# Attention gradients for 32 batches on one core: two heads of dV stored as 120 and 8 rows in every second batch, and o for two batches at once as 104 and 24 rows

## The chip, the cores and the metric

The kernel runs on one core of a Trainium2 chip. A core has engines that run side by side, each with its own list of instructions: TensorE (PE, with its weight loads PEld), VectorE (DVE), ScalarE (ACT), GpSimd (POOL) and SyncE (SP). SP and POOL also issue DMA transfers between the large memory (HBM) and the core's own memory (SBUF). Sixteen DMA engines carry the packets of all these transfers. The metric is the device time of one execution in microseconds; lower is better.

## The reference

Inputs are q and grad_out with shape (32, 32, 4, 128) and k and v with shape (32, 4, 2048, 128), all bf16. It is grouped-query softmax attention: eight query heads share one of four key/value heads. The outputs are o and the three gradients.

```python
k = jnp.repeat(k, rep, axis=1)                # rep = 8
v = jnp.repeat(v, rep, axis=1)
scores = jnp.einsum("bhqd,bhkd->bhqk", q, k) * scale
p = softmax(scores, axis=-1)
o = jnp.einsum("bhqk,bhkd->bhqd", p, v)
# returned: o, and the gradients dq, dk, dv of o against grad_out
```

With dO for grad_out and delta the row sums of dO times o: dV is p transposed times dO; dP is dO times V transposed; dS is p times (dP minus delta); dQ is dS times K, and dK is dS transposed times Q, both with the scale.

## The kernel before, in words

The unit of work is a batch. Its 32 query heads with 4 rows each are the 128 rows of one tile; its 2048 keys are 16 chunks for each of 128 rows, so that one SBUF row holds 16 keys of each of the four heads. k, v, dK and dV of one batch are each 128 rows x 4 heads x 16 chunks x 128 values, which is 2 MB, and a row of one head is 4 KB long.

A batch is cut into named pieces: `LK` and `LV` load k and v by SP's queue, one transfer of 512 KB a head. `QDT`, `KT0` to `KT7` and `VT0` to `VT7` transpose through TensorE, and DVE copies the result out of PSUM. `Sa`, `Sb` make the scores and their maxima, `EXa`, `EXb` the exponentials on ACT. `NRM` (line 234) sums them on DVE, takes the reciprocal `rinv`, and has GpSimd write the scaled operands `dop` (grad_out times `rinv`) and `qp` (q times the scale), four instructions each (line 231). `ETa`, `ETb` transpose the exponentials, `O` multiplies them with v, scales the result into `o_sb`, stores it, and forms delta. `dPa`, `dPb` form dS, `dSTa`, `dSTb` transpose it, `dQ` makes and stores dq. `dV0` to `dV7` and `dK0` to `dK7` (function `outer`) multiply, and ACT copies each piece into a tile of the batch; when the eighth piece is in, two transfers by GpSimd's queue store the tile, 1 MB and two heads each (line 326). The last batch is stored by halves of the chunks (line 319).

The order of all pieces is written out by hand: `HEAD` for the first iterations, `STEADY` for one iteration in the middle, `TAIL` for the end. An iteration mixes the pieces of three batches: a `-` behind a name means the batch before, `+` the batch after, `+2` the one after that. In the steady iteration of batch b, the instructions of GpSimd come in this order: dop and qp of b (`NRM`), the store of dq of b-1, two stores of dk of b-1, the store of o of b, in every fourth iteration (b = 1, 5, 9, ..., 25) two loads of q and grad_out for four batches (`GROUP`, line 142, called by `LK`), and two stores of dv of b. Then comes dop of b+1.

The program gives each transfer of GpSimd's queue the next of eight semaphores, in rotation, and the transfer waits until the transfer that had that semaphore before, the eighth one back, has landed. GpSimd waits in order: what stands behind such a wait in its list, dop of the next batch too, waits with it. A transfer's semaphore is raised by one by each of the sixteen DMA engines when its share is done; the trace has the time of each of these sixteen steps.

Tiles come from pools: four buffers for dV and dK together (`out_pool`), three each for `o_sb` and `dq_sb` (`io_pool`).

## Time and profile before

| what | value |
|---|---|
| median of three runs | 701.2 us (699.08, 701.2, 701.52) |
| the profiled execution | 698.71 us |
| its span, from the first instruction to the last | 696.7 us |
| mean granted TensorE clock | 0.98 |
| PE busy, DVE busy, ACT busy | 90%, 84%, 82% of the span |
| POOL busy | 43% of the span |
| moved by DMA | 274.44 MB, mean 394 GB/s |
| POOL's transfers, from issue to landing (median) | dv 23.6 us, dk 22.1 us, o 23.2 us, dq 16.2 us |
| SP's transfers, from issue to landing (median) | k 13.8 us, v 18.6 us |

The profile is a page made from one execution. It has the busy time of each engine, the span in 40 slices with the bytes per second that were moved, the DMA queues, and the chain of work that ended last, followed back from the last instruction. Beside the page, the trace can be asked for the instructions in a window of time, the waits of one engine, and each transfer's issue and landing. In the chain and the timeline the first number is the start in microseconds from the span's start and the second the duration. "q0" are the transfers that GpSimd issued, "q1" those of SP, and "q8" and "q14" fetch the program's own instructions.

### The profile page before, as it was taken

How to read it: one execution, taken by the hardware profiler on the slowest of the kernel's cores; microseconds unless marked ns; L12 is line 12 of the kernel's file. 1: busy time of each engine (PE TensorE's matmuls, PEld its weight loads, DVE VectorE, ACT ScalarE, POOL GpSimd, SP SyncE). 2: the span in 40 equal slices, each digit the busy share in tenths (PEclk: the TensorE clock that was granted, in tenths of full speed). 3: DMA queues.
4: the chain of work that ended last, by engine and by line, in shares of the span. 5: the costliest groups of instructions: out<-in, count | busy, mean ns of one | idle time of the engine just before them, and what ended most of it. 6: DMA issues, size and time to landing. Idle time of an engine off the chain costs nothing.

```text
span 696.7 us, 28064 instructions
## 1 busy us (share of the span) xinstructions
PE 626.0 (90%) x12352; PEld 454.1 (65%) x12352; DVE 584.5 (84%) x992; ACT 569.1 (82%) x673; POOL 302.7 (43%) x506
## 2 busy tenths in 40 slices
PE   5899999999998989979999798998998889998982
PEld 4577776677676656666666676667766677666661
DVE  5999999999997998869988688888988869898960
ACT  0698989899887989869888687887888868888994
POOL 1355443555454435443354424544434543345452
PEclk9999999999999999999999899999999989999997
DMA  9989999999999999999999999999999999999767
GB/s 339 400 317 411 417 415 416 416 413 415 417 415 417 414 417 416 417 409 412 415 415 413 373 397 398 400 410 382 416 416 417 415 340 393 415 414 415 289 257 274
DMA packets 75577, 274.44 MB, mean 394 GB/s; under 512 B 8448, under 2 KB 8448, under 8 KB 75456
## 3 DMA queue, kind: packets, MB, share of 16 engines
q0 software_dynamic: 37536, 138.16, 49.3%
q1 hardware_dynamic: 37920, 134.50, 48.9%
q8 instruction: 96, 1.57, 0.8%
q14 instruction: 25, 0.20, 0.1%
HBM read 136.31 MB, written 136.31 MB: 391 GB/s over the span
## 4 chain that ended last, share of the span: by engine, by line
PE 43%; DMA 33%; ACT 6%; DVE 5%; POOL 5%; issue 5%; SPq 0%; POOLq 0%; DVEq 0%; ACTq 0%
PE banks L181 18%; DMA k_sb<-in_k_dram 15%; DMA out_dram<-dk 12%; PE banks L303 10%; PE banks L264 7%; ACT dv L307 5%; PE banks L248 5%; DMA out_dram<-dv 4%; PE banks L198 3%; POOL dop L231 2%; DMA v_sb<-in_v_dram 2%; DVE kt L183 2%; DVE ds L338 1%; ACT dk L307 1%; POOL qp L231 1%
## 5 line engine op out<-in xcount | busy, mean ns | idle before, releaser
L307 ACT CAST dv<-banks 128x1024 bf16<-128x1024 f32 x256 | 245.5, 1028 | 56.9 <-PE banks L303 56.3
L307 ACT CAST dk<-banks 128x1024 bf16<-128x1024 f32 x256 | 250.7, 1025 | 34.5 <-PE banks L303 23.6
L183 DVE COPY kt<-banks 128x1024 bf16<-128x1024 bf16 x256 | 164.3, 680 | 8.3 <-PE banks L181 8.3
L183 DVE COPY vt<-banks 128x1024 bf16<-128x1024 bf16 x256 | 166.2, 680 | 1.3 <-PE banks L181 0.9
L181 PE MATMUL banks<-ident,k_sb 128*128 128x128 bf16 x2048 | 145.8, 221 | 13.1 <-DMA k_sb<-in_k_dram 8.6
L181 PE MATMUL banks<-ident,v_sb 128*128 128x128 bf16 x2048 | 143.5, 220 | 14.3 <-ACT dv L307 9.7
L231 POOL TENSOR_SCALAR dop<-do_sb,rinv 32x128 bf16<-32x128 bf16 x128 | 76.7, 599 | 181.3 <-PE banks L303 118.9
L181 PEld LDWEIGHTS <-k_sb 128*128 128x128 bf16 x2048 | 120.8, 99 | 41.9 <-issue 31.7
L181 PEld LDWEIGHTS <-v_sb 128*128 128x128 bf16 x2048 | 122.2, 98 | 28.7 <-issue 23.3
L303 PE MATMUL banks<-dop,e 64*128 64x256 bf16 x1024 | 99.3, 276 | 15.1 <-POOL dop L231 11.3
L326 POOL DMA_DIRECT2D out_dram<-dv x62 | 43.7, 709 | 138.0 <-ACT dv L307 67.6
L338 DVE SCALAR_TENSOR_TENSOR ds<-banks,delta,e 128x1024 bf16<-128x1024 f32 x64 | 82.2, 1284 | 17.3 <-PE banks L198 14.3
L303 PE MATMUL banks<-qp,ds 64*128 64x256 bf16 x1024 | 86.4, 272 | 2.1 <-ACT dk L307 1.4
L231 POOL TENSOR_SCALAR qp<-q_sb,srinv 32x128 bf16<-32x128 bf16 x128 | 78.1, 610 | 10.7
L222 ACT ACTIVATE e<-banks,negb 128x1024 bf16<-128x1024 f32 x64 | 70.7, 1111 | 8.6 <-DVE negb L214 8.5
L211 DVE TENSOR_REDUCE m<-banks 128x1 f32<-128x1024 f32 x64 | 75.1, 1215 | 0.9 <-PE banks L198 0.9
L303 PEld LDWEIGHTS <-e 64*128 64x128 bf16 x1024 | 34.0, 94 | 63.1 <-issue 46.7
L250 DVE COPY et<-banks 128x1024 bf16<-128x1024 bf16 x64 | 41.3, 686 | 29.6 <-PE banks L248 29.6
L303 PEld LDWEIGHTS <-ds 64*128 64x128 bf16 x1024 | 42.2, 94 | 28.8 <-ACT dv L307 13.1
L326 POOL DMA_DIRECT2D out_dram<-dk x62 | 44.0, 713 | 13.6 <-DMA out_dram<-dk 13.0
L250 DVE COPY dst<-banks 128x1024 bf16<-128x1024 bf16 x64 | 43.5, 681 | 5.5 <-PE banks L248 3.6
L248 PE MATMUL banks<-ident,ds 128*128 128x128 bf16 x512 | 39.4, 221 | 7.1 <-ACT dk L307 6.8
(39 smaller groups left out, 484.1 us busy)
## 6 DMA issues: line engine op xcount, KB each, us to landing
k_sb<-in_k_dram SPq DMA_DIRECT2D x128, 512.0 KB, 13.8
v_sb<-in_v_dram SPq DMA_DIRECT2D x128, 512.0 KB, 18.6
out_dram<-dv POOLq DMA_DIRECT2D x64, 1024.0 KB, 23.6
out_dram<-dk POOLq DMA_DIRECT2D x64, 1024.0 KB, 22.1
out_dram<-o_sb POOLq DMA_DIRECT2D x32, 32.0 KB, 23.2
out_dram<-dq_sb POOLq DMA_DIRECT2D x32, 32.0 KB, 16.2
q_sb<-in_q_dram POOLq DMA_DIRECT2D x7, 128.0 KB, 21.9
do_sb<-in_grad_out_dram POOLq DMA_DIRECT2D x7, 128.0 KB, 22.0
```

Of the source, the lines that this page charges most:

```text
L181: nc.tensor.transpose(out=ps[:, 4 * hh + j, :], in_=S[which][:, 2 * (i % 2) + hh, 4 * (i // 2) + j, :], identity=ident[:])
L183: nc.vector.tensor_copy(out=S[f"{which}t{i}"][:], in_=ps)
L211: nc.vector.reduce_max(out=S["m"][:, i:i + 1], in_=S[f"s{i}"][1], axis=AX.X)
L222: nc.scalar.activation(out=S[f"e{i}"][:], in_=ps, func=ACT.Exp, bias=S["negb"][:], scale=scale, accum_out=S["l"][:, i:i + 1],)
L231: nc.gpsimd.tensor_scalar(out=t[r, h % 2, :], in0=src[r, :], scalar1=by[r, :], scalar2=None, op0=ALU.mult)
L248: nc.tensor.transpose(out=ps[:, u, :], in_=S[f"{src}{i}"][:, P * u:P * u + P], identity=ident[:])
L250: nc.vector.tensor_copy(out=S[f"{name}{i}"][:], in_=ps)
L264: nc.tensor.matmul(ps[G * h:G * h + G, :], lhsT=S[f"{xt}{c // 8}"][:, c % 8, G * h:G * h + G], rhs=S[kv][:, h, c, :], start=(c == 0), stop ...
L303: nc.tensor.matmul(ps[:, a, :, c, :], lhsT=S[f"{x}{i // 4}"][r, u:u + P], rhs=S[y][r, :, :], start=True, stop=True, tile_position=(2 * G * ...
L307: copy(out=S[name][:, :, 2 * i:2 * i + 2, :].rearrange("p h c d -> p h (c d)"), in_=banks.ap(t).rearrange("p a (j w) -> p (a j) w", j=2),)
L326: store.dma_start(out=dst[b][:, 2 * a:2 * a + 2, :], in_=o[:, 2 * a:2 * a + 2].rearrange("p h c d -> p h (c d)"))
L338: nc.vector.scalar_tensor_tensor(out=S[f"ds{i}"][:], in0=ps, scalar=S["delta"][:], in1=S[f"e{i}"][:], op0=ALU.subtract, op1=ALU.mult,)
```

## The change

Three things change, all in what GpSimd's queue is given.

- dV: in every odd batch (the last one excepted) the second transfer, heads 2 and 3, is cut into one of rows 0 to 119 and one of rows 120 to 127. In batch 0 heads 2 and 3 are stored as two transfers of 120 rows, one a head, and one of 8 rows for both.
- o: from batch 2 on, o of an even batch stays in SBUF, and with the odd batch behind it two transfers store both batches: rows 0 to 103 and rows 104 to 127. Batches 0 and 1 are stored singly as before.
- `io_pool` has two buffers instead of three; the one for o now holds two batches.

Over two steady iterations GpSimd's queue issues 5 transfers in the even one (dq, dk, dk, dv, dv) and 8 in the odd one (dq, dk, dk, o of 104 rows, o of 24 rows, dv, dv of 120 rows, dv of 8 rows), where it issued 6 and 6. The two loads of `GROUP` fall into odd iterations, between o and dv, before and after. In all GpSimd issues 222 transfers instead of 206. The order of the instructions on every engine is otherwise the same, SP's list included, and so are the bytes.

```diff
--- before.py
+++ after.py
@@ -102,7 +102,7 @@
     ds_pool = ctx.enter_context(tc.tile_pool(name="dsp", bufs=2))
     dst_pool = ctx.enter_context(tc.tile_pool(name="dstp", bufs=2))
     out_pool = ctx.enter_context(tc.tile_pool(name="outp", bufs=4))
-    io_pool = ctx.enter_context(tc.tile_pool(name="iop", bufs=3))
+    io_pool = ctx.enter_context(tc.tile_pool(name="iop", bufs=2))
     qd_pool = ctx.enter_context(tc.tile_pool(name="qdp", bufs=2))
     sm_pool = ctx.enter_context(tc.tile_pool(name="smp", bufs=3))
     ps_pool = ctx.enter_context(tc.tile_pool(name="ps", bufs=1, space=bass.MemoryType.PSUM))
@@ -270,14 +270,20 @@
     def O(b):
         S = st[b]
         t, ps = gathered(S, "et", "v")
-        o_sb = io_pool.tile([P, D], BF16, name="o_sb")
-        nc.vector.tensor_scalar(out=o_sb[:], in0=ps, scalar1=S["rinv"][:], scalar2=None, op0=ALU.mult)
-        banks.give(t)
-        store.dma_start(out=o_f[b], in_=o_sb[:])
+        if b % 2 == 0:
+            st["o"] = io_pool.tile([P, 2, D], BF16, name="o_sb")
+        o_sb = st["o"][:, b % 2, :]
+        nc.vector.tensor_scalar(out=o_sb, in0=ps, scalar1=S["rinv"][:], scalar2=None, op0=ALU.mult)
+        banks.give(t)
+        if b < 2:
+            store.dma_start(out=o_f[b], in_=o_sb)
+        elif b % 2:
+            for r in (slice(0, 104), slice(104, P)):
+                store.dma_start(out=o_f[b - 1:b + 1, r].rearrange("w p d -> p w d"), in_=st["o"][r])
         junk = sm_pool.tile([P, D], BF16, name="junk")
         S["delta"] = sm_pool.tile([P, 1], FP32, name="delta")
         nc.vector.tensor_tensor_reduce(
-            out=junk[:], in0=o_sb[:], in1=S["do"], scale=1.0, scalar=0.0,
+            out=junk[:], in0=o_sb, in1=S["do"], scale=1.0, scalar=0.0,
             op0=ALU.mult, op1=ALU.add, accum_out=S["delta"][:],
         )
 
@@ -322,8 +328,16 @@
                 )
         elif S[name + "left"] == 0:
             o = S.pop(name)
+
+
             for a in range(2):
-                store.dma_start(out=dst[b][:, 2 * a:2 * a + 2, :], in_=o[:, 2 * a:2 * a + 2].rearrange("p h c d -> p h (c d)"))
+                parts = [(slice(0, P), slice(2 * a, 2 * a + 2))]
+                if name == "dv" and a and b == 0:
+                    parts = [(slice(0, 120), slice(2, 3)), (slice(0, 120), slice(3, 4)), (slice(120, P), slice(2, 4))]
+                elif name == "dv" and a and b % 2:
+                    parts = [(slice(0, 120), slice(2, 4)), (slice(120, P), slice(2, 4))]
+                for r, h in parts:
+                    store.dma_start(out=dst[b][r, h, :], in_=o[r, h].rearrange("p h c d -> p h (c d)"))
 
     def dV(b, i, copy=nc.scalar.copy):
         outer(st[b], "e", "dop", dv_v, "dv", i, b, copy)
```

## The prediction

> **What bounds the kernel now.** I read the page first, then the busy time by stage, then the chain of waits, GpSimd's timeline, and last the sixteen semaphore steps of each transfer in the trace.
>
> ```profile
> span 696.7 us, 28064 instructions
> ...
> GB/s 339 400 317 411 417 415 416 416 413 415 417 415 417 414 417 416 417 409 412 415 415 413 373 397 398 400 410 382 416 416 417 415 340 393 415 414 415 289 257 274
> ...
> q0 software_dynamic: 37536, 138.16, 49.3%
> q1 hardware_dynamic: 37920, 134.50, 48.9%
> ```
>
> The moved bytes stand on a plateau of 415 GB/s, with dips (373, 340) and a tail. A 4 KB packet takes 159 ns in the trace; sixteen engines of that pace move 412 GB/s, so on the plateau all sixteen work. By stage:
>
> ```profile
> core 0: us, PE busy (x) PEld busy (x) DVE busy (x) ACT busy (x) POOL busy (x), PEclk, DMA share, GB/s
> ...
> 200.00:300.00 100.00, 90.71 (x1807) 65.00 (x1803) 88.33 (x149) 84.61 (x101) 46.00 (x76) 1.00 1.03 415
> ...
> 384.00:408.00 24.00, 20.44 (x366) 14.12 (x363) 15.99 (x28) 15.96 (x20) 9.27 (x16) 0.86 0.98 371
> 557.00:579.00 22.00, 20.16 (x362) 14.94 (x363) 15.09 (x27) 15.45 (x19) 9.40 (x16) 0.85 0.93 339
> ```
>
> In the dips PE, DMA and the granted clock (0.85) fall together. The chain of waits says what happens there:
>
> ```profile
> 534.93 25.95 DMA out_dram<-dv
> ...
> 561.45 0.71 POOL out_dram L326
> 562.16 4.10 issue
> ...
> 566.28 0.72 POOL out_dram L326
> 567.00 0.09 issue
> 567.09 0.60 POOL dop L231
> ```
>
> GpSimd waits for the landing of a store issued 26 us earlier, the eighth one back; the second dv store waits 4.1 us more, and dop of the next batch stands behind it. GpSimd's timeline and PE's show the same at 388 us, in the next iteration with the two q and grad_out loads:
>
> ```profile
> 382.73 0.76 POOL L142 DMA_DIRECT2D q_sb<-in_q_dram  x1 [4.08 <-DMA out_dram<-dk]
> ...
> 388.60 0.71 POOL L326 DMA_DIRECT2D out_dram<-dv  x1 [4.37 <-ACT dk L307]
> 393.42 0.72 POOL L326 DMA_DIRECT2D out_dram<-dv  x1 [4.11 <-DVE kt L183]
> 394.23 2.63 POOL L231 TENSOR_SCALAR dop<-do_sb,rinv 32x128 bf16<-32x128 bf16 x4
> ```
>
> ```profile
> 391.92 1.20 PE L181 MATMUL banks<-ident,v_sb 128*128 128x128 bf16 x16
> 395.55 0.27 PE L303 MATMUL banks<-dop,e 64*128 64x256 bf16 x1 [2.43 <-POOL dop L231]
> 396.91 0.58 PE L303 MATMUL banks<-dop,e 64*128 64x256 bf16 x3 [1.10 <-POOL dop L231]
> ```
>
> The names DVE and ACT in the brackets were long done; dv of 361.71 and 362.40 landed at 388.02 and 393.13.
>
> Why do stores take 26 us? The sixteen steps of one dv store, from its issue to the first, eighth, fifteenth and sixteenth engine: issued at 92.67, 10.3, 12.7, 14.6, 14.7 us; at 254.34, 11.0, 19.0, 21.1, 26.0; at 410.87, 7.2, 8.3, 10.6, 26.5; at 600.73, 7.6, 8.4, 9.9, 26.2. So late in the run one engine of sixteen is some 16 us behind all others. In the stage with loads alone (issues at 8.67 to 17.60 us) the gap between the last two steps stays at 0.80 to 0.81 us; it grows only once stores run.
>
> **The change part by part.** The sum is made for the profiled execution, 698.7 us: span 696.7 and 2.0 around it. It lies 0.4% below the median of 701.2.
>
> *120 and 8 rows.* A 128-row transfer gives each engine 8 rows. I take it that 120 rows go to fifteen engines with 8 each, and one engine gets none. That saves it 8 rows x 2 heads = 16 packets of 4 KB; the 8-row transfer may give 2 back to it. At 159 ns that is 2.2 to 2.5 us per two batches, 33 to 38 us over 15 odd batches. The late engine lacks 16 us by 600 us, and the others ran dry for some 10 us more in the dips (the slices 409 to 382 and 340, 393 lack 242 of 416 GB/s, each 17.4 us). So the dose fits what that one engine lacks, 26 us, if it is the one spared. The other fifteen get at most 2 packets, 0.3 us, per two batches.
>
> What it is worth if so: first, the landing is then that of the fifteenth step. dop's lateness behind rinv after the five late iterations with loads was 1.6, 3.3, 4.3, 1.9 and 2.7 us, 13.7 in sum. Timing the new list by the fifteenth steps of before, I get 3.1, 3.2, 0.8, 0 and 0: 7.2. Second, the pace. dop starts at 199.13 in batch 9 and at 628.85 in batch 29: 429.7 us, 21.5 an iteration. An iteration moves 8.52 MB (four times 2.1 MB and the small ones), at 415 GB/s 20.5 us. Twenty of these and 7.2 us make 417.2, so 12.5 us less. Bounds: 0 (all of it hidden) to 21.5 (20.4 at 418, no stall).
>
> *The row's cost in a 15-way transfer* is not in this trace. A gain is excluded, as no row shows 4 KB in fewer than 159 ns. From above, slowed 4 KB packets at 200 us take 182 to 196 ns: 16 an engine x 28 ns x 15 = 7 us. I take 0, as 95% of the packets keep 159 ns, and keep 7 for the range.
>
> *One more issue.* 0.71 us in odd batches (line 326), one after dv's second store. The time from there to dop is free where nothing waits: the second dv store of batch 15 ends at 342.41, rinv of the next batch is there at 348.4, so 6 us cover 0.71. Without that cover each 0.71 us would reach PE, since dop ends 0.03 to 0.7 us ahead of its first matmul: 15 x 0.71 = 11 us.
>
> *The eight semaphores.* This is the part that speaks against the change. With 5 and 8 transfers (10 with loads) eight back is another transfer. In plain odd batches the 8-row store waits for the second dv store of the batch before; with loads, for the first dk store of its own iteration. In batch 15 that store landed at 350.56 (fifteenth step 341.90), while dop started at 348.60: 3.0 us late with the lag, in time without. In batch 17 dk of 375.62 landed at 398.48 (fifteenth 388.70), with dop due at 389.95: 9.6 us late with the lag, against 4.3 now, and 0.8 without. This is in the 7.2 above. Other waits (SP's list, PE) gain none.
>
> *o for two batches, and two buffers.* Two stores of o become two of other shapes, with the same 256-byte rows. An o buffer is written again three batches after its store, 60 us, a dq buffer after two, 42 us; o lands after 25.8 us and dq after 17.9 at that stage. No cost; the cover goes if a landing exceeds 42 us.
>
> Sum: 698.7 - 12.5 = 686.2; with half the distance to the median, 687 us.
>
> [...]
>
> **The rivals.** *The spared engine is not the late one.* No row names an engine, so nothing proves which share is left out. Then every landing stays at the sixteenth step and the new semaphore waits bite. By before's landings dop is late in batches 9, 13, 17, 21 and 25 by 7.0, 8.6, 9.6, 7.4 and 8.1 us, 40.7 against 13.7: 27 us more, 726 us. Plain odd batches add up to 4.2 each: in all 64.6 against 13.7, 750 us. I take 726, since stalls shorten the queue (22.0 us instead of 26.3 after the stall at 388). It decides once a dv store takes over 27 us, as from 250 us on.
>
> *The lag is cured and nothing is gained.* PE and ACT are 90% and 82% busy, and up to 180 us an iteration took 19.5 us at the same 415 GB/s. If the others' queues merely fill, 15 x 0.71 us of issues and the 7 us eat the 12.5: 698 to 702 us.
>
> *15-way transfers are so slow* that the spared time comes back in other engines: doubling 240 packets' time costs 16 x 159 ns x 15 = 38 us; a part of it is 705 to 720.
>
> **How the numbers follow.** Forecast 0.53: 678 to 695 us, since the dose fits and a whole share is left out. Wrong engine 0.35; nothing gained 0.06; slow transfers 0.06. A measurement here tells 0.5%, 3.5 us, from no change. Faster 0.53, same 0.06, slower 0.41. The range 678 to 728 holds the forecast's cases but 0.03, the third and fourth, and half of the wrong engine's.
>
> **What would show it.** Right: a dv store's fifteenth and sixteenth steps within some 3 us late in the run, landings near 15 us, no "4.10 issue" in front of dop, a plateau to 640 us. Wrong: the last gap still grows to 10 us or more, the 8-row store is issued after rinv of the next batch, and PE idles for dop in every odd iteration. It would also be wrong if 4 KB packets grew beyond 159 ns.

## The result: slower by 1.1%

The changed kernel takes 708.78 us (median of five runs, 705.23 to 710.9) against 700.34 us for the kernel before (699.08 to 701.52). The ratio is 1.0112, with a 95% interval of 1.007 to 1.0153. The prediction said 687 us and faster; the time lies inside its range, but on the other side of no change. The profiled execution took 708.78 us, 706.9 of them the span. Of all runs below, two executions of the kernel called start 1 were in the chip's slower state and are left out of its median and ratio. (One number of the description above has to be put right: GpSimd issues 223 transfers after the change, not 222.)

First the page of the changed kernel. The lines are the span, the bytes per second in forty slices, the two large queues, the shares of the chain that ended last, the group of dV matmuls that wait for `dop`, and the median landings of loads and stores.

```profile
span 706.9 us, 28119 instructions
...
GB/s 339 389 308 389 411 415 416 415 412 415 414 416 410 384 402 380 412 413 416 416 411 414 373 379 402 384 416 409 412 401 369 415 386 407 408 408 413 262 223 264
...
q0 software_dynamic: 38320, 138.17, 49.1%
q1 hardware_dynamic: 37920, 134.50, 48.5%
...
PE 68%; issue 8%; ACT 8%; DVE 5%; DMA 5%; POOL 4%; SPq 0%; POOLq 0%; ACTq 0%; DVEq 0%
...
L309 PE MATMUL banks<-dop,e 64*128 64x256 bf16 x1024 | 101.2, 278 | 25.4 <-POOL dop L231 20.5
...
k_sb<-in_k_dram SPq DMA_DIRECT2D x128, 512.0 KB, 11.2
v_sb<-in_v_dram SPq DMA_DIRECT2D x128, 512.0 KB, 15.7
...
out_dram<-dv POOLq DMA_DIRECT2D x48, 1024.0 KB, 18.4
out_dram<-dv POOLq DMA_DIRECT2D x15, 960.0 KB, 21.8
out_dram<-dv POOLq DMA_DIRECT2D x16, 64.0 KB, 17.9
```

The large transfers land sooner than before: k after 11.2 us (13.8 before), v after 15.7 (18.6), whole dv stores after 18.4 (23.6). The kernel is slower all the same. The slices say where: the plateau of 415 is still there, but it has more holes (384, 402, 380 from 230 us on, 373 and 379 from 389 us on).

The slices can be turned into time. Each slice lacks (416 - GB/s) / 416 of its length. Before the change the first three slices lack 8.0 us, the 34 in the middle 11.0, the last three 17.9; with 274.44 MB at 416 GB/s, 659.7 us, that makes the span of 696.7. After the change it is 9.0, 17.0 and 21.2. So the middle lost 6.0 us and the end 3.3. It also shows something that should have been seen in advance: 11.0 us was all that the middle had to give, and the forecast counted on 12.5.

The stages, by windows (the columns are the stretch, its length, and the busy time of PE, weight loads, DVE, ACT and POOL, then PE's granted clock, the DMA share and GB/s):

```profile
200.00:300.00 100.00, 89.26 (x1792) 64.39 (x1788) 81.49 (x141) 79.86 (x95) 46.45 (x76) 0.95 1.01 400
208.00:232.00 24.00, 16.52 (x296) 12.24 (x294) 17.03 (x28) 14.98 (x19) 8.54 (x13) 0.92 1.02 409
384.00:408.00 24.00, 18.53 (x349) 13.71 (x350) 15.60 (x27) 14.85 (x19) 9.25 (x16) 0.88 0.98 381
557.00:579.00 22.00, 18.35 (x358) 13.56 (x354) 16.01 (x28) 15.86 (x19) 10.39 (x17) 0.94 1.02 402
```

From 200 to 300 us, where the kernel before had no hole (415 GB/s), there is one now. From 208 to 232 us PE is busy for 16.5 of 24 us while the DMA engines are still full; the hole in the bytes follows after that, when the loads that PE's progress would have released are missing (SP's loads of k wait for PE's matmuls by 337.5 us in sum, up to 13.5 at a time). GpSimd's timeline of that stretch (start, duration, engine, line, operation; in brackets the idle time before it and what ended it):

```profile
207.82 0.62 POOL L296 DMA_DIRECT2D out_dram<-dq_sb  x1
208.44 1.42 POOL L340 DMA_DIRECT2D out_dram<-dk  x2
209.86 1.35 POOL L282 DMA_DIRECT2D out_dram<-o_sb  x2
213.86 0.78 POOL L142 DMA_DIRECT2D q_sb<-in_q_dram  x1 [2.65 <-DMA out_dram<-dk]
218.91 0.77 POOL L142 DMA_DIRECT2D do_sb<-in_grad_out_dram  x1 [4.27 <-DMA out_dram<-dv]
225.92 1.47 POOL L340 DMA_DIRECT2D out_dram<-dv  x2 [6.24 <-issue]
229.44 0.57 POOL L340 DMA_DIRECT2D out_dram<-dv  x1 [2.05 <-DMA out_dram<-dk]
230.09 2.62 POOL L231 TENSOR_SCALAR dop<-do_sb,rinv 32x128 bf16<-32x128 bf16 x4
```

The store at 229.44 is the new one of 8 rows. With ten transfers in an iteration that has the loads, the eighth one back is the first dk store of the same iteration, issued at 208.44 and landed at 229.15. `dop` of batch 10 stands behind it. Its input `rinv` was there at 221.62, so `dop` is 8.3 us late; before the change it was 1.6. PE, in the same stretch:

```profile
223.60 1.05 PE L181 MATMUL banks<-ident,v_sb 128*128 128x128 bf16 x16
231.40 0.37 PE L309 MATMUL banks<-dop,e 64*128 64x256 bf16 x1 [6.75 <-POOL dop L231]
232.76 0.58 PE L309 MATMUL banks<-dop,e 64*128 64x256 bf16 x3 [0.99 <-POOL dop L231]
```

That is a stall of 7.7 us where PE had none of more than 2.43 us in the piece shown of before. Added over all iterations, `dop` is late by 22.7 us (13.7 before): 8.3 us in batch 10, 5.8 in 18, 3.5 in 26, 2.0 in 22, 1.9 in 14, 1.1 in 6.

PE's idle gaps of more than 0.15 us between 22 and 650 us, by what ended them:

| PE waits for | before, us | after, us |
|---|---|---|
| `dop` (GpSimd) | 11.3 | 20.5 |
| nothing that the profile shows | 9.5 | 15.1 |
| ACT's copies of dV | 9.3 | 9.8 |
| ACT's copies of dK (an output buffer) | 6.8 | 0.2 |
| loads of k and v | 7.0 | 0.4 |

So the sooner landings did pay: 6.6 us for buffers and 6.6 us for loads are gone. `dop` took 9.2 us back, and the second row 5.6. In all, the rows of the table grew by 2.1 us only, and the span by 10.2. PE's own busy time grew by 3.6 us (626.0 to 629.6), at a granted clock of 0.975 against 0.980, and the rest lies outside the window. By the starts of `dop`, the loss falls between batches 9 and 13 (90.2 us against 84.2) and between 29 and 31 (42.2 against 38.3); between 13 and 17 and between 25 and 29 the changed kernel is the faster one by 2 to 3 us. The gaps of that row end 1.2 to 1.6 us after a 16 KB packet of the queue q8, which fetches instructions. The end of the kernel has one more of them, in the chain (start, duration, what):

```profile
660.52 0.27 PE banks L181 x3
660.80 3.44 issue
664.24 0.89 PE banks L181 x13
```

It too ends 1.4 us after such a packet, and it is about as long as the 3.3 us that the last slices lost.

### The profile page after: what moved, and what is told of

Read it like the earlier page. It is cut to its first block, busy times and chain, and to the rows that moved or that the text cites. A ratio compares the mean times of both kernels' runs of the same rounds, so it can differ in the third digit from the quotient of the medians.

```text
span 706.9 us, 28119 instructions
## 1 busy us (share of the span) xinstructions
PE 629.6 (89%) x12352; PEld 456.2 (65%) x12352; DVE 584.6 (83%) x992; ACT 569.3 (81%) x673; POOL 317.0 (45%) x523
## 2 busy tenths in 40 slices
DMA packets 76361, 274.44 MB, mean 388 GB/s; under 512 B 9337, under 2 KB 9517, under 8 KB 76240
## 4 chain that ended last, share of the span: by engine, by line
PE 68%; issue 8%; ACT 8%; DVE 5%; DMA 5%; POOL 4%; SPq 0%; POOLq 0%; ACTq 0%; DVEq 0%
PE banks L181 28%; PE banks L309 17%; PE banks L264 8%; PE banks L198 7%; PE banks L248 7%; ACT dv L313 6%; DMA out_dram<-dv 3%; POOL dop L231 2%; POOL out_dram L340 2%; DVE kt L183 2%; DVE ds L352 1%; ACT dk L313 1%; DVE vt L183 1%; DVE m L211 1%; DMA v_sb<-in_v_dram 1%
## 5 line engine op out<-in xcount | busy, mean ns | idle before, releaser
L181 PEld LDWEIGHTS <-k_sb 128*128 128x128 bf16 x2048 | 122.4, 99 | 40.9 <-issue 37.0
L340 POOL DMA_DIRECT2D out_dram<-dv x79 | 53.8, 685 | 177.9 <-ACT dv L313 104.5
L309 PE MATMUL banks<-dop,e 64*128 64x256 bf16 x1024 | 101.2, 278 | 25.4 <-POOL dop L231 20.5
L352 DVE SCALAR_TENSOR_TENSOR ds<-banks,delta,e 128x1024 bf16<-128x1024 f32 x64 | 82.2, 1284 | 19.7 <-PE banks L198 17.1
L309 PE MATMUL banks<-qp,ds 64*128 64x256 bf16 x1024 | 88.3, 273 | 2.3 <-ACT dk L313 1.4
L222 ACT ACTIVATE e<-banks,negb 128x1024 bf16<-128x1024 f32 x64 | 70.7, 1110 | 12.2 <-DVE negb L214 12.2
L309 PEld LDWEIGHTS <-ds 64*128 64x128 bf16 x1024 | 43.8, 94 | 28.6 <-ACT dv L313 12.6
L198 PE MATMUL banks<-vt,qdt 128*32 128x512 bf16 x512 | 42.1, 398 | 1.2 <-issue 1.0
## 6 DMA issues: line engine op xcount, KB each, us to landing
k_sb<-in_k_dram SPq DMA_DIRECT2D x128, 512.0 KB, 11.2
v_sb<-in_v_dram SPq DMA_DIRECT2D x128, 512.0 KB, 15.7
out_dram<-dk POOLq DMA_DIRECT2D x64, 1024.0 KB, 16.5
out_dram<-dv POOLq DMA_DIRECT2D x48, 1024.0 KB, 18.4
out_dram<-dv POOLq DMA_DIRECT2D x16, 64.0 KB, 17.9
```

Source lines behind the costliest of these rows:

```text
L181: nc.tensor.transpose(out=ps[:, 4 * hh + j, :], in_=S[which][:, 2 * (i % 2) + hh, 4 * (i // 2) + j, :], identity=ident[:])
L198: nc.tensor.matmul(ps[G * h:G * h + G, a, :], lhsT=S["qdt"][:, col, G * h:G * h + G], rhs=xt[:, 4 * (h % 2):4 * (h % 2) + 4, :].rearrange( ...
L222: nc.scalar.activation(out=S[f"e{i}"][:], in_=ps, func=ACT.Exp, bias=S["negb"][:], scale=scale, accum_out=S["l"][:, i:i + 1],)
L309: nc.tensor.matmul(ps[:, a, :, c, :], lhsT=S[f"{x}{i // 4}"][r, u:u + P], rhs=S[y][r, :, :], start=True, stop=True, tile_position=(2 * G * ...
L340: store.dma_start(out=dst[b][r, h, :], in_=o[r, h].rearrange("p h c d -> p h (c d)"))
L352: nc.vector.scalar_tensor_tensor(out=S[f"ds{i}"][:], in0=ps, scalar=S["delta"][:], in1=S[f"e{i}"][:], op0=ALU.subtract, op1=ALU.mult,)
```

## The experiments

Theory A is the prediction's: the late DMA engine costs time, and sparing it gives time. Its rivals (B, later W and U) say that the extra transfers and their waits, or the uneven shares, decide. All ratios are to the kernel before on the same chip. Executions of one kernel differ by up to 10 us (start 3: 702.06 to 712.55), so what is read from one trace explains where time goes, and the ratios say how much. The runs of the next part were on one chip; starts 1 to 4 on a second; start 5, its variant and the two other kernels behind it on a third; the first four kernels with a moved store on a fourth, and the last two kernels on a fifth.

### The dealing taken back in steps

First, the two 120-row stores of batch 0 go. By the author's count they shift the dealing of all later shares by six (15, 15 and 8 shares are six more than two rounds of sixteen), so without them another engine should be the spared one. That the shares go round in turn was an assumption here.

```diff
-                if name == "dv" and a and b == 0:
-                    parts = [(slice(0, 120), slice(2, 3)), (slice(0, 120), slice(3, 4)), (slice(120, P), slice(2, 4))]
-                elif name == "dv" and a and b % 2:
+                if name == "dv" and a and b % 2:
```

> The changed kernel with dv of batch 0 stored by two transfers of 128 rows again; the cuts of 120 and 8 and of 104 and 24 rows in later batches stay. In the trace of the changed kernel the late engine carries 16 packets of every 120-row transfer (its step comes 4.9 to 5.3 us after that of the transfer before), so it is not the spared one; a 104-row transfer made 13 packets of 4 KB and a 24-row one 12 packets of 1 KB, so the shares go to 13 and 12 engines, and the sum of 15, 8, 13 and 12 is 48, three full rounds. Without the 15 + 15 + 8 of batch 0 the spared engine should be another one, ten further on in the round. Theory A (the spared engine was the wrong one, and the one spared now is the late one): the gap between the fifteenth and the sixteenth step stays under 4 us to the end, 690 us (684 to 697). Theory B (it is still another one): the gap grows to 6 to 10 us as in the changed kernel, 705 to 711 us. Theory C (the late engine is late because of its backlog alone and sparing does nothing): as B.

Measured: 706.59 us (706.08 to 710.55), ratio 1.0103 (1.0071 to 1.0136). The 16th step of a 120-row store comes 4.4 to 6.6 us after that of the transfer before (2.7 in the last), as for a 128-row store; in the changed kernel it is 5.0 us in each of the three read here (issued at 226.63, 265.12 and 309.45 us: 5.03, 4.98, 4.99), against 4.83 to 5.25 for the whole dk and dv stores issued between 208 and 309 us, one of 2.77 aside. The last engine is therefore not the spared one in either. One thing moved: from batch 7 to 27 the last step of the 8-row store now comes 0.64 to 1.14 us after the one before, mostly 0.8 to 0.9, where the changed kernel has 0.40 to 0.49. By these steps the last engine carries two packets of it here and none there. (In the first batches no single engine is clearly last yet, and the steps are mixed in both.)

Second, the same number of transfers, but in halves, meant to give all sixteen engines the same.

```diff
-            for r in (slice(0, 104), slice(104, P)):
+            for r in (slice(0, 64), slice(64, P)):
...
-                    parts = [(slice(0, 120), slice(2, 4)), (slice(120, P), slice(2, 4))]
+                    parts = [(slice(0, 64), slice(2, 4)), (slice(64, P), slice(2, 4))]
```

> The same number of transfers in the same places as in the changed kernel, but cut as 64 and 64 rows (dv of odd batches, o of two batches), and in batch 0 as 128, 64 and 64 rows, so that each engine gets the same number of rows. Theory A (the loss comes from the eight semaphores, as a transfer more in odd batches makes GpSimd wait for later landings, and sparing a wrong engine does nothing): 705 to 713 us, dop of batches 10, 14, 18, 22 and 26 late by 2 to 9 us as in the changed kernel. Rival (the loss comes from transfers over 15, 13, 12 or 8 engines): 699 to 702 us.

Measured: 704.71 us, ratio 1.0053 (1.0019 to 1.0087). `dop` is late by 22.5 us in sum, 6.4 of them in batch 10. The time lies between the two expectations. About half of the loss comes without the uneven cuts, from the transfers alone; the interval overlaps a little with that of the run before.

Third, the part of the change that saves a transfer: o of two batches in one store of 128 rows, dV as before the change.

```diff
-            for r in (slice(0, 104), slice(104, P)):
+            for r in (slice(0, P),):
```

> The part of the change that only lessens the transfers: o of two batches in one transfer of 128 rows, dv stored as before; 11 transfers in two batches instead of 12. Theory A (the rotation of semaphores sets the stalls): the batches with loads wait for a transfer that was issued earlier, so dop is late by less than the 13.7 us in sum of the kernel before, 692 to 699 us. Rival (the number of transfers does not matter): 699 to 702 us.

Measured: 696.91 us (696.45 to 697.25), ratio 0.9952 (0.9934 to 0.9971). It is faster than both kernels, though one engine is late as before, by up to 17.5 us. `dop` is late by 7.5 us in sum. PE's waits (what waited, for what: us in total, times, the longest) show what is next in line:

```profile
PE banks L181 <- DMA k_sb<-in_k_dram: 21.4, 19, 1.9
PE banks L181 <- ACT dv L313: 10.5, 30, 0.5
PE banks L309 <- POOL dop L231: 5.1, 6, 1.1
```

Fourth, `dop`'s stalls taken away by another road: the kernel before with its loads of q and grad_out on SP's queue, so that GpSimd issues six transfers in every iteration.

```diff
-            GROUP(b // W + 1, nc.gpsimd)
+            GROUP(b // W + 1, nc.sync)
```

> The kernel before with the loads of q and grad_out issued by SP's queue instead of GpSimd's, so that no iteration has eight transfers of GpSimd's. It measures what the stalls in the batches with loads cost. Theory A: dop is no longer late in batches 10, 14, 18, 22 and 26 (13.7 us in sum before), 687 to 695 us, and the gap of the last engine still grows past 10 us. Rival (DMA alone is the bound, the stalls only move time): 698 to 702 us.

Measured: 713.57 us (710.41 to 716.37), ratio 1.0195 (1.015 to 1.024). `dop` is late by 0.4 us in the whole run and the gap between the last two engines is at most 5.9 us. Neither expectation held. Both things that the prediction wanted to cure are cured, and the kernel is slower than any other here. PE's waits, and the longest in its timeline:

```profile
PE banks L181 <- DMA k_sb<-in_k_dram: 32.8, 12, 9.1
```

```profile
230.51 0.61 PE L181 MATMUL banks<-ident,k_sb 128*128 128x128 bf16 x4 [9.09 <-DMA k_sb<-in_k_dram]
```

The loads now stand in front of k in SP's list, and PE waits for k instead. So this run does not say what the cures would be worth without that wait.

### Does any start spare the late engine, and does it pay?

If the dealing goes round in turn, each transfer starting at the engine behind the last one's (the cursor), the place of the spared engine can be moved. Four kernels cut o of batch 0 so that, by the author's count, the start should move by one to four from that of the first experiment. That count was an assumption, and the packets of batch 0, below, do not bear it out.

```diff
-            store.dma_start(out=o_f[b], in_=o_sb)
+            for r in (slice(0, 90), slice(90, P)) if b == 0 else (slice(0, P),):
+                store.dma_start(out=o_f[b, r], in_=o_sb[r])
```

The other cuts are 121 and 7, 102 and 26, 114 and 14 rows.

> [...] Theory A (a late engine that is fixed): in exactly one of the four the late engine's step of a 120-row transfer comes within 1 us of the step before it, and its gap stays under 4 us; this one takes 688 to 699 us, the other three 704 to 712. Theory B (the start is not the same in every execution, or another engine becomes late once this one is spared): none of the four is under 702 us.

> [...] Theory A: one of the four has a gap under 4 us and 688 to 699 us. Theory B: all 702 to 712 us.

> [...] Theory A: one of the four has a gap under 4 us and 688 to 699 us. Theory B: all 702 to 712 us.

> [...] Theory A: one of the four has a gap under 4 us and 688 to 699 us. Theory B: all 702 to 712 us.

Measured: 705.7 us (ratio 1.0043 to 1.0143), 707.65 (1.0085 to 1.0134), 709.36 (1.0104 to 1.0156) and 708.35 (1.0064 to 1.0188). In all four the 16th engine carries the 120-row store (4.3 to 6.6 us up to batch 27) and, from batch 7 on, two packets of the 8-row one (0.6 to 0.9 us, mostly 0.8). `dop` of batch 10 is late by 7.6 to 8.6 us in each. In the second the gap between the last two engines is at most 3.4 us after 480 us, and it gains nothing by it.

The fifth start was chosen from these steps: if each cut moves the start as counted, only one place of the late engine fits the 8-row steps of all these kernels, and this start should spare it. It cuts o of batch 0 into 40 and 88 rows. Four kernels ran with it, two of them in the next part.

> The sixth start. In the starts 0, 1, 2, 3 and 4 the late engine carries the 8-row transfer (its last step comes 0.8 us after that of the transfer before), in the changed kernel (start 6) it does not (0.4 us). If the shares are dealt in turn, the 8-row transfer goes to the eight engines from the spared one on; only one engine fits all six traces, and it is the one that start 5 spares. So in this kernel the last step of a 120-row transfer should come less than 1.5 us after the one before, and the 8-row step 0.8 us or more. Theory A (the prediction's: a spared late engine pays for the extra transfers): gap between the 15th and 16th step at most 3 us, dv landing in 15 to 18 us, 687 to 697 us. Theory B (the rotation of eight semaphores and the extra transfers set the loss, and the lag is not what sets the time): the dose fits and the gap shrinks, but dop of batch 10 is still 6 to 9 us late and the time is 703 to 710 us.

Measured: 710.98 us (705.75 to 712.16), ratio 1.0166 (1.0141 to 1.0191). No gain, and the expected step did not come: the 16th engine still carries the 120-row store (4.7 to 5.9 us after the one before, up to batch 27), and 0.6 to 0.8 us for the 8-row one. The gap between the last two is 6.9 us at most. The time is a microsecond above theory B's range.

The packets of batch 0 say why: the start did not move. The 38 rows of start 1 had been counted as two shares. In its trace they are twelve packets of 768 bytes (three rows of 256), one of 516 (two rows and 4 bytes) and three of 12 bytes. That fits the rows divided by 16 and rounded up for each engine, until no rows are left. The cuts of the other starts fit this too: the 40 rows of start 5 are 13 packets of three rows and one with a single row. So these plain stores were shared out otherwise than the strided stores of 120, 104 and 24 rows, and, by the steps that follow, did not move the start.

The later steps agree. In the first experiment and in all five starts the last engine carries the 120-row and the 8-row store, and its step in the 104-row store is mostly 0.35 to 0.38 us, too short for that store's 4 KB share (0.47 to 0.50 us for most o stores of the kernel with dV cut alone, below, where each engine gets 4 KB). By the count of shares, only three engines are in the 8-row store and out of the 104-row one; had the start moved by one to four, these would be three other engines in start 4 than in start 1, which ran on the same chip.

So none of the five starts spared the late engine, and whether sparing it pays was not tested. They are the first experiment over again with one more store in batch 0. These six kernels, on three chips, have ratios of 1.0093 to 1.0166, so differences below 0.7 points between kernels on different chips have to be read with care.

> Start 5 with dq of two batches in one transfer, so that two iterations have 12 transfers again, as before the change (5 and 7 instead of 6 and 6; with loads 9). In iterations with loads the 8-row store still waits for the first dk store of its own iteration. Theory A: the spared engine now costs nothing extra: 684 to 694 us. Theory B: dop of batch 10 still 6 us late or more, 696 to 705 us: some 5 us less than start 5, because four iterations with loads and all plain ones wait for older transfers.

```diff
-        dq_sb = io_pool.tile([P, D], BF16, name="dq_sb")
-        nc.scalar.activation(out=dq_sb[:], in_=ps, func=ACT.Copy, scale=S["srinv"][:])
+        if b % 2 == 0:
+            st["dq"] = io_pool.tile([P, 2, D], BF16, name="dq_sb")
+        nc.scalar.activation(out=st["dq"][:, b % 2, :], in_=ps, func=ACT.Copy, scale=S["srinv"][:])
...
-        store.dma_start(out=dq_f[b], in_=dq_sb[:])
+        if b % 2:
+            store.dma_start(out=dq_f[b - 1:b + 1].rearrange("w p d -> p w d"), in_=st["dq"][:])
```

(A scratch tile, `junk`, gets one buffer instead of three to make room.) Measured: 708.34 us, ratio 1.012 (1.0083 to 1.0158). `dop` of batch 10 is late by 7.2 us, 26.3 in sum. With the transfer count of before the loss is still there, so the count alone is not the cause. (The start did not move in this kernel either.) Both theories expected a lower time.

> o and dq each for two batches in one whole transfer, dV as before the change: 10 transfers in two iterations where there were 12. No engine is spared. Theory B: fewer transfers move the eight-back wait to older ones, dop is late by under 5 us in sum, and the time is 690 to 696 us, at or below that of o pairs alone (696.9). Theory A: the lag still reaches 15 us and more and every landing with it, so no better than o pairs alone: 696 to 702 us.

Measured: 699.95 us, ratio 0.9997 (0.9986 to 1.0009). `dop` is late by 0.4 us in the whole run, as theory B said, yet the kernel is slower than with o in pairs alone. PE's waits for k grow (page, the k transposes: 33.3 us idle, 24.8 with o in pairs alone). The time is in theory A's range, with a lag of 12.2 us at most. Fewer transfers do not go on paying; why k comes later with dq in pairs was not settled.

> dV cut into 120 and 8 rows, with o of two batches in one whole transfer, 12 transfers in two iterations as before the change. The shares of two iterations now add up to 7 more than a whole turn, so the spared engine changes each time, and the late one is spared once or twice in 15 at most. In iterations with loads the 8-row store waits for dq, not dk, of its own iteration, which lands about 5 us earlier. Theory A: no engine is relieved, nothing is gained: 699 to 704 us, with gaps of 8 us or more. Theory B: against o pairs alone (696.9) one more transfer in odd iterations and a wait for dq: 698 to 703 us, dop of batch 10 late by 2 to 5 us. The two agree on the time; apart from theory A, a time at 704.7 us or above would say that uneven dealing as such costs, whatever the rotation.

```diff
                 parts = [(slice(0, P), slice(2 * a, 2 * a + 2))]
+                if name == "dv" and a and b % 2:
+                    parts = [(slice(0, 120), slice(2, 4)), (slice(120, P), slice(2, 4))]
```

Measured: 700.26 us, ratio 1.0004 (0.9988 to 1.002), in the range that both theories gave. Against o in pairs alone, the cut of dV costs 0.5 points. `dop` of batch 10 is late by 1.8 us: here the 8-row store waits for dq of its own iteration, which lands earlier than dk.

The steps of this kernel also bear on how shares are dealt. By the count, two iterations deal seven shares more than whole turns, so the window of eight engines that get the 8-row store should move by seven each time. The last engine's step in the 8-row stores of batches 1, 3, ... 27 comes after the one before by 0.82, 0.40, 0.81, 0.87, 0.48, 0.81, 0.49, 0.84, 0.47, 0.79, 0.49, 0.40, 0.87, 0.47 us. An engine that stands at place 5 of the window in batch 1, then at 14, 7, 0, 9, 2, 11, 4, 13, 6, 15, 8, 1, 10 of sixteen, is inside the window (0 to 7) in just those of the fourteen cases where the step is about 0.8, and outside where it is 0.4 to 0.5. Place 0 is the engine that the 120-row store spares, and in that batch, 7, its step in the 120-row store comes after 2.41 us instead of some 5. So the fourteen steps fit shares of 16, 15 and 8 that are dealt on from where the last ones ended. The place 5 was chosen to fit; no other of the sixteen fits more than twelve. The fifteenth step, of batch 29, is 0.36 us where the count would give 0.8; the queues run empty there (the last three slices of the changed kernel move 223 to 264 GB/s), and in every kernel that step is 0.2 to 0.5. So one engine is last through this run, and it was spared once. That is read from the pattern: the trace names no engine.

### The wait in front of `dop`

The last dv store of an odd batch is now issued behind `dop` and `qp` of the next batch, in four kernels: start 5, the changed kernel, start 5 with dq in pairs, and the even one with halves.

```diff
+    held = []
...
         paired(S, "qp", S["q"], S["srinv"], b)
+        while held:
+            store.dma_start(**held.pop())
...
-                for r, h in parts:
-                    store.dma_start(out=dst[b][r, h, :], in_=o[r, h].rearrange("p h c d -> p h (c d)"))
+                for n, (r, h) in enumerate(parts):
+                    args = dict(out=dst[b][r, h, :], in_=o[r, h].rearrange("p h c d -> p h (c d)"))
+                    if b and n:
+                        held.append(args)
+                    else:
+                        store.dma_start(**args)
```

> Start 5, with the 8-row store issued behind dop and qp of the next batch. Theory A (a spared late engine pays, the wait hid it): dop of batch 10 under 3 us late, 687 to 695 us, clearly below the even kernel of this call. Theory W (the wait in front of dop was the loss, the lag is worth nothing): dop in time likewise, 697 to 702 us, the same as the even kernel. Theory U (uneven shares cost by themselves: seven engines carry 18 packets where 16 is even, 0.32 us in each pair of batches, 4.8 us over 15 pairs): 3 to 5 us above the even kernel.

> The changed kernel with the same move: its spared engine is not the one that is late before the change. Theory A: no relief, 699 to 704 us, above start 5 by 8 us or more. Theory W: 697 to 702 us, the same as start 5 and the even kernel. Theory U: 3 to 5 us above the even kernel, as start 5.

> As start 5 deferred, with dq of two batches in one transfer: 12 transfers in two iterations, as before the change, and the 120-row store waits for one of the iteration before it in iterations with loads, no longer for dq of its own. Theory A: 685 to 692 us. Theory W: 695 to 700 us, near o and dq pairs alone (699.9). Theory U: 700 to 705 us.

> The even kernel (64 and 64 rows, no engine spared, the same transfers) with its last dv store issued behind dop and qp of the next batch. All theories: dop of batch 10 under 3 us late. Theory W: the loss of 3.7 us is gone, 697 to 702 us. If it stays at 703 us or above, the wait in front of dop is not what costs, and the count of transfers is left.

The even kernel first. GpSimd's timeline without the move:

```profile
224.01 1.31 POOL L340 DMA_DIRECT2D out_dram<-dv  x2 [4.68 <-ACT dq_sb L294]
229.12 0.62 POOL L340 DMA_DIRECT2D out_dram<-dv  x1 [3.80 <-DMA out_dram<-dk]
229.82 2.62 POOL L231 TENSOR_SCALAR dop<-do_sb,rinv 32x128 bf16<-32x128 bf16 x4
```

and with it:

```profile
223.86 1.31 POOL L348 DMA_DIRECT2D out_dram<-dv  x2 [4.74 <-ACT dk L317]
225.25 2.62 POOL L233 TENSOR_SCALAR dop<-do_sb,rinv 32x128 bf16<-32x128 bf16 x4
227.96 0.21 POOL L244 TENSOR_SCALAR srinv<-rinv 128x1 f32<-128x1 f32 x1
228.27 2.65 POOL L233 TENSOR_SCALAR qp<-q_sb,srinv 32x128 bf16<-32x128 bf16 x4
230.97 0.67 POOL L247 DMA_DIRECT2D out_dram<-dv  x1
```

`dop` starts at 225.25 instead of 229.82, still 3.7 us late where under 3 was expected. In the changed kernel it is 5.3 us late, in start 5 6.3, in start 5 with dq in pairs 3.5: where o is two stores and dq one a batch, the store of dv in front of `dop` is now the ninth and waits for dq of its own iteration. Measured times, the ratios without and with the move:

| kernel | `dop` waits behind the last store | last store moved behind `dop` | time moved, us |
|---|---|---|---|
| even halves | 1.0053 (1.0019 to 1.0087) | 0.9994 (0.9977 to 1.0012) | 700.06 |
| the changed kernel | 1.0112 (1.007 to 1.0153) | 1.0057 (1.003 to 1.0084) | 703.56 |
| start 5 | 1.0166 (1.0141 to 1.0191) | 1.013 (1.0093 to 1.0166) | 709.76 |
| start 5, dq in pairs | 1.012 (1.0083 to 1.0158) | 1.0116 (1.008 to 1.0151) | 707.39 |

In the even kernel the loss goes with that wait: the two intervals do not meet, though narrowly and on two chips, and the time is that of the kernel before. In sum `dop` is still 18.0 us late there (22.5 without the move, 13.7 before the change). In the changed kernel the same move takes 0.55 points, half of the loss, with intervals that just overlap. In start 5 with dq in pairs it takes nothing, though `dop` is late by 15.9 us in sum instead of 26.3; so a `dop` that comes sooner does not always shorten the time. The even kernel is in theory W's range and the changed one in U's; the two with start 5 are above every range. Start 5 is the slowest of the four, 9.7 us above the even kernel where A had it clearly below, but that does not settle A: the late engine is not spared there, and the last one lags by up to 12.7 us. Start 5 and the changed kernel, on one chip, differ by 0.7 points with intervals apart. The last engine carries two packets of each 8-row store in start 5 and none in the changed kernel, so a rival remains that no run isolates: what counts may be how much the late engine carries, as theory A has it, and not how even the shares are.

What stays, 0.6 points between the changed and the even kernel with the move, on one chip, goes with the uneven cuts of dV and o. Two runs ask whether it matters that it is always the same engine. They leave dV at 120 and 8 rows and cut o in halves, so that by the count the spared engine moves by seven from pair to pair.

```diff
-            for r in (slice(0, 104), slice(104, P)):
+            for r in (slice(0, 64), slice(64, P)):
```

> The changed kernel with o cut as 64 and 64 rows instead of 104 and 24: the same transfers in the same order and number, dV as 120 and 8 rows, but two iterations deal 55 shares, 7 more than whole turns, so another engine is spared each time. Theory U (always sparing the same engine costs, since the same seven engines carry 2 packets more each time): as the even kernel, 702 to 706 us. If the 15-way transfer or the 8-row one costs by itself: as the changed kernel, 707 to 711 us.

> The same with the 8-row store behind dop and qp of the next batch. Theory U: as the even kernel with the same move, 698 to 701 us. If the 15-way transfer costs by itself: 702 to 706 us, as the changed kernel with that move.

Measured: 705.44 us, ratio 1.0066 (1.004 to 1.0092), and with the move 703.32 us, 1.0036 (1.0018 to 1.0054). Both lie between the even kernel and the changed one. With the move, the moving 120 and 8 rows are slower than even halves by 0.4 points, intervals narrowly apart, and the time is in the range of the second expectation: the uneven cut seems to cost something wherever the spared engine is, but the two kernels ran on different chips. That the same engine is always spared may cost 0.2 to 0.5 points more, but there the intervals overlap, and it stays open. In both runs 13 of the first fourteen 8-row steps fit one place that moves as above, and in batch 23, where that place is spared, the step of the 120-row store is 2.34 and 2.44 us.

## Why the prediction was wrong

**Which engine is spared.** The step that the forecast rested on, "the dose fits what that one engine lacks, 26 us, if it is the one spared", failed on its condition: in the changed kernel the 16th step comes some 5 us after the one before in 120-row and 128-row stores alike. The first rival had this right. That the place left out moves on with the shares dealt fits the first fourteen steps of the kernel with dV cut alone: 0.79 to 0.87 us where the late engine would be inside the window that moves by seven, 0.40 to 0.49 where it would be outside.

**What sparing it is worth.** This stays open: no run spared the late engine in every pair of batches. What the runs do show is that the term of -12.5 us was too large before any engine was spared. It set twenty iterations of 20.5 us (8.52 MB each, 170.4 MB) against the 429.7 us between 199.13 and 628.85; the trace of before moves 174.3 MB in that time. At 415 GB/s that is 420.0 us, so 9.7 us were to be had there and not 19.7, and 2.5 of them beside the 7.2 us of stalls that the sum kept; by the slices the whole middle lacked 11.0. Nor is a small lag enough: it is at most 5.9 us with the loads on SP's queue and 3.4 late in the run with start 2, and both kernels are slow, with other waits in the way, while the fastest kernel has a lag of 17.5 us. The third rival, the lag cured and nothing gained, was not tested either.

**The shares of the others.** The prediction noted that "the other fifteen get at most 2 packets, 0.3 us, per two batches" and charged nothing. A pair of batches gives seven engines 18 packets where 16 is even, 0.32 us at 159 ns a packet, and where all sixteen are busy that may be a price: by the author's estimate 4.8 us over 15 pairs, if these seven bound the pace. Measured is 0.6 points, 3.5 us in the medians, between the changed and the even kernel once the wait is out of the way. The size fits; that this is the mechanism was argued, not isolated, and the packets that the late engine itself carries are the rival.

**The eight semaphores.** Named as the part that speaks against the change, with the right waits: the 8-row store waits for the first dk store of its own iteration. The size was wrong in the forecast. By the fifteenth steps it had 3.1 us for batch 10; the run has 8.3, and even the fifteenth step of that dk store (226.65 us) came 5.0 us after `rinv`. So less than a third of this wait (2.5 us) was a matter of the last engine. By the even kernel and the changed one with the move, about half of the loss goes with this wait.

**The first rival's time.** 726 us was too much by 17 us. It had `dop` late by 7.0, 8.6, 9.6, 7.4 and 8.1 us in the five late iterations with loads; measured are 8.3, 1.9, 5.8, 2.0 and 3.5. It kept before's landings of 22 to 26 us. Each stall drains the queues: the six large stores behind the stall at 229 us land after 12.3 to 20.2 us, and the waits for k, v and output buffers (13.2 us) disappeared. The prediction saw that stalls shorten the queue but put no number on it.

**Right as predicted.** The 120-row store goes to fifteen engines, as the count of 4-byte packets below has it. Where the late engine is spared once (batch 7 of the kernel with dV cut alone), its step takes 2.41 us instead of 5.0, so the dose of some 2.5 us was right. 4 KB packets keep their 159 ns (median of both queues, before and after), though just 159 ns are 88% of before's packets and not 95%, and a few take less (0.14%, the shortest 156 ns). The extra issue of 0.7 us is hidden in plain odd batches: `dop` is never more than 0.3 us late there. Two buffers for o and dq cost no wait: in the changed kernel no wait of DVE or ACT is put down to a landing.

**Not foreseen at all.** PE's gaps that nothing shows grew by 5.6 us, and by 3.4 at the end; PE's busy time grew by 3.6 us at the lower granted clock.

## What to carry to other kernels

Turn the slices of the profile into missing time before summing gains: what the plateau lacks in a stage is the most that a cure of that stage can give while the plateau itself stays. A transfer added to a queue with rotating semaphores waits for a different transfer in every iteration of another length, so look for the oldest one still in flight and keep what the compute engines need ahead of it; with one store moved behind `dop`, the even cut ran as the kernel before. Shares that spare one engine load the others, and where all are busy that may not be free (120 and 8 rows against even halves, with the store moved: 1.0036 against 0.9994, on two chips). Saving a transfer paid once (o of two batches in one whole store, 0.9952) and not a second time (dq as well, 0.9997). Before a run is read as a test, look in its trace whether the edit did what it was meant to do: the packet sizes of the five starts show that the start had not moved.

## What the runs showed of the hardware

- In the changed kernel a strided store does not always go to all sixteen engines: 104 rows of two batches are 13 packets of 4 KB, 24 rows 12 packets of 1 KB, and by the 4-byte packets of the next item 120 rows leave one engine out and 8 rows eight. The steps of the kernel with dV cut alone fit shares that are dealt on from where the last ones ended (fourteen of fifteen steps). The plain stores of o of batch 0 in the five starts came out otherwise: the rows over 16, rounded up, until none are left (38 rows: twelve packets of three rows, one of two).
- Every transfer still has sixteen steps (all 464 before, all 481 after), and the packets fit 4 bytes for each row that an engine lacks. The changed kernel has 45 packets of 64 bytes and 60 of 16, three and four for each of the fifteen pairs of o stores, as many as engines are left out there. It has 4,080 packets of 4 bytes against 3,296 before: 272 for the sixteen steps of 17 more transfers, and 512 that match one for each 4 KB row that an engine lacks (256 for the 120-row stores, 256 for the 8-row ones). A spared engine is not through at once: in batch 7 of the kernel with dV cut alone its step still takes 2.41 us. Sixteen packets of the other queue at 159 ns would be 2.5 us; that this is what the time goes to is the author's estimate.
- By the pattern of its steps, one and the same engine is last through the run with dV cut alone. In the kernel before the last step of a store comes up to 19.3 us after the fifteenth.
- PE stands still for 7.1 us (o in pairs alone), 9.5 (before), up to 22.6 us (start 5) in sum with no wait in sight, each time until 1.2 to 1.6 us after a 16 KB packet of the queue that fetches instructions. There are 96 of these packets before and after, against 24,704 matmuls and weight loads of PE, 257 to a packet; so the amount fetched is the same. That the fetching is the cause was read from the times alone. The gaps that end behind such packets add up to 9.5 us before and 15.1 after, between 22 and 650 us.
